# The first MoE's second matmul in rounded high and low parts one token tile earlier, in a fused kernel of scan, MoE and routed MoE

## The chip, the cores and the metric

The kernel is one program on one NeuronCore of a Trainium2 chip. The core has a matrix engine (TensorE, rows of the profile call it PE, its weight loads PEld), a vector engine (DVE), an activation engine (ACT), GpSimd (POOL) and a queue engine (SP) that starts most DMAs. Each engine works through its own instruction queue in order; semaphores tie the queues together. The metric is device time in microseconds, lower is better. The engines' times below are microseconds from the start of the span, unless ns is written.

## The reference

Three stages run one behind the other on 3072 tokens (4 sequences of 768) of width 256. The first is a gated linear scan with 8 heads, in chunks of 32. Its output goes to a dense MoE, and that to a routed MoE with 8 experts, of which each token takes the best one:

```
h = x @ w_in                     # 3072x256 @ 256x2048
g = h * np.cos(h)
x = g @ w_out                    # 3072x2048 @ 2048x256
...
logits = x @ w_gate
expert_idx = np.argmax(logits, axis=1)
...
h = np.maximum(np.einsum('ecd,edf->ecf', disp, w1), 0.0)
y = np.einsum('ecf,efd->ecd', h, w2)
...
out[i] = gate_w[i] * y[expert_idx[i], pos[i]]
```

The change concerns `x = g @ w_out`.

## The kernel before

**The first MoE.** The 3072 tokens are six tiles of 512 (`NT` = 6), and the 2048 hidden columns are 16 blocks of 128 (`NF` = 16). One block of one tile is an *item*, 96 in all; items 0 to 15 are tile 0, items 16 to 31 tile 1, and so on. For each item PE computes h (`mm1`, line 919, six matmuls of 512 columns in fp32r into the PSUM tile `hp`, of which there are three). Then ACT rounds (`c_round`, line 926, into one of six buffers named `g`), DVE takes the fraction (`c_frac`, line 930), ACT takes the sine (`c_sin`, line 933) and DVE multiplies by h (`c_mul`, line 936), which also gives `hp` back.

**The second matmul** (`mm2`) adds the item to the tile's output `yt`. It has two forms. For items below `SPLIT0` it is plain fp32: two matmuls of `w_out` on g (line 962), which the trace shows as four records. From `SPLIT0` on ACT first makes a rounded copy of g in fp32r, the high part (`c_hi`, line 940, tile `gh`), then `c_lo` (line 945) subtracts it to make the low part (`gw`, a buffer of the ring of `g`), and `mm2` is six fp32r matmuls (line 957: four on `gh`, two on `gw`) on `w_o`, which holds w_out in high and low parts. Before, `SPLIT0` is 32: tiles 0 and 1 are plain.

**What runs beside it.** The scan works in 12 groups of 256 tokens, about two for each tile (`a_...`). Per group ACT switches its table, takes an exponential of 2304 columns (line 644) and switches back (ACT_TABLE_LOAD rows at 644 and 933). w_in and w_out are loaded into `pre`, joined from words by DVE (`w_c1` to `w_c3`, lines 871 to 881) into `w_f`, a view of the memory that later holds `w1a`, and split into high and low parts (w_in: 890 on ACT, 894 on POOL; w_out: `w_ohi` 899 on ACT, `w_olo` 903 on POOL). `w_o` takes the memory of `pre`. After each tile its routing runs (`r_evac` evacuates `yt` at 970 and 976, `r_x2` matmuls at 990 and 992, `r_cp` 1006 and 1009, and more), and the expert weights are scaled and split (1229 to 1254) for the routed MoE, which takes the last 150 us or so.

**What sets the order.** The table `PLACE` gives every step, by name, a number for each of its occurrences; the steps are sorted by it and issued in that order. Each engine's queue holds its share of that one list.

Of the kernel before, what the change touches and what calls it, by code (L numbers as in the profile page):

```python
# [28 lines left out]
    'ass': [484, 563, 675, 815, 911, 1033, 1162, 1258],  # L29
# [51 lines left out]
    'chi': [617, 636, 640, 664, 666, 687, 712, 723, 739, 753, 763, 789, 790, 810, 826, 825, 869,  # L81
# [6 lines left out]
    'clo': [629, 658, 652, 677, 682, 713, 727, 729, 751, 776, 769, 794, 804, 812, 828, 842, 877,  # L88
# [5 lines left out]
    'con': [102],  # L94
    'cp': [176, 321, 371, 452, 597, 684, 801, 927, 1073, 1206],
    'css': [1500, 1536, 1580, 1604, 1640, 1655, 1683, 1723],
# [5 lines left out]
    'dfi': [236, 205, 243, 220, 342, 279, 297, 326],  # L102
    'et': [1377],
    'et2': [1393],
    'ete': [1416],
    'ets': [1402],
    'ett': [1406],
    'ex': [94, 115, 116, 151, 118, 233, 334, 362, 345, 430, 516, 545, 559, 667, 721, 830, 770,
        931, 928, 1047],
    'ex0': [1450],  # L110
    'ex1': [1623],
    'exp': [159, 260, 344, 444, 562, 679, 800, 908, 1028, 1157],
    'frc': [136, 146, 172, 190, 196, 209, 224, 240, 255, 281, 287, 306, 304, 313, 349, 360, 381,
# [6 lines left out]
    'gat': [138, 230, 323, 429, 540, 649, 798, 906, 1017, 1158],  # L120
    'id': [1469],
    'in0': [1475],
    'in1': [1629],
    'iv0': [1474],
    'iv1': [1732, 1737, 1742],
    'lt': [1552],
    'lte': [1610],
    'lts': [1568],
    'ltt': [1587],
# [203 lines left out]
def fused_kernel(ctx: ExitStack, tc: tile.TileContext, I, out: bass.AP):  # L333
# [10 lines left out]
    NF = 16  # L344
# [119 lines left out]
    at = at_cm.__enter__()  # L464
# [1267 lines left out]
    used = []  # L1732
# [77 lines left out]
```

## Time and profile before

| what | before |
|---|---|
| median of 3 runs | 575.1 us (573.28 to 575.87) |
| the profiled execution | 572.15 us |
| its span, first to last instruction | 570.4 us |
| PE busy | 533.9 us (94%) |
| DVE, ACT, POOL busy | 407.7 (71%), 371.5 (65%), 341.8 (60%) us |
| mean granted TensorE clock | 0.985 |

The share of PE is high over nearly all of the span, but matmul records overlap and their ends are modelled, so a busy PE may still wait a little between matmuls. A row of the chain of waits is one step of the work that ended last, followed back from the end of the program; a "window" row gives busy time of each engine in a stretch.

### The profile page before, as it was taken

Reading aid. Unit: us, or ns where it says so; the run is one execution under the profiler, and the core shown is the slowest. Engines: PE = TensorE matmul, PEld = TensorE weight load, DVE = VectorE, ACT = ScalarE, POOL = GpSimd, SP = SyncE. Lnnn points to the kernel's source line nnn. Section 1 sums busy time; section 2 is a strip of 40 time slices with the busy share of each in tenths; the row PEclk is TensorE's granted clock in tenths of the full one; section 3 lists DMA queues with packets and bytes.
Section 4 is the critical chain, followed back from the end, with each engine's and each line's share of the span. In section 5 each row is a group of like instructions: output and inputs, shape, how many; then the busy total and the mean of one; then the engine's idle time right before and its main releaser. Section 6 shows DMA issues by size and latency. Waiting matters only on the chain.

```text
span 570.4 us, 10385 instructions
## 1 busy us (share of the span) xinstructions
PE 533.9 (94%) x3156; PEld 385.5 (68%) x3156; DVE 407.7 (71%) x869; ACT 371.5 (65%) x675; POOL 341.8 (60%) x414
## 2 busy tenths in 40 slices
PE   8968999999999899999999997996989999999993
PEld 7635666666677678878888885674657665666672
DVE  7889985657876987699788799989966723333441
ACT  4638997684779597978798895787679622232220
POOL 6775152558558869776964773787568444322454
PEclk9999999999999999999999998999889999999997
DMA  7896744396263365326422231456897778777882
GB/s 241 260 328 234 235 146 126 119 333 196 95 203 114 110 203 185 130 81 197 153 70 75 75 110 39 130 144 176 187 206 189 127 147 152 141 143 117 155 171 63
DMA packets 110645, 89.91 MB, mean 158 GB/s; under 512 B 64542, under 2 KB 99424, under 8 KB 110592
## 3 DMA queue, kind: packets, MB, share of 16 engines
q1 hardware_dynamic: 107808, 82.26, 53.3%
q0 software_dynamic: 2784, 6.97, 5.0%
q8 instruction: 30, 0.49, 0.4%
q14 instruction: 23, 0.19, 0.1%
HBM read 59.50 MB, written 15.54 MB: 132 GB/s over the span
## 4 chain that ended last, share of the span: by engine, by line
PE 54%; DVE 17%; ACT 13%; DMA 9%; issue 5%; POOL 1%; SPq 0%; DVEq 0%; ACTq 0%; POOLq 0%
PE hp L919 16%; PE yt L962 8%; PE hp L1601 8%; PE yp L1648 7%; PE yt L957 7%; DMA ht<-hr 5%; DVE g L936 2%; DMA out_dram<-yacc,scat 2%; ACT g L933 2%; DVE g L930 2%; PE bcp L698 2%; ACT g L926 2%; DMA wst<-in_w_dram 1%; PE ypg L824 1%; PE sp L745 1%
## 5 line engine op out<-in xcount | busy, mean ns | idle before, releaser
L919 PE MATMUL hp<-xT,w_in 128*128 128x512 f32 x576 | 158.4, 414 | 6.7 <-DVE g L936 5.8
L919 PEld LDWEIGHTS hp<-xT,w_in 128*128 128x128 f32 x576 | 105.5, 189 | 39.7 <-DVE g L936 11.3
L945 POOL TENSOR_TENSOR gw<-g,gh 128x512 fp32r<-128x512 f32 x64 | 85.9, 1347 | 45.3 <-ACT gh L940 21.1
L933 ACT ACTIVATE g<-g,halfpi 128x512 f32<-128x512 f32 x96 | 68.2, 717 | 25.0 <-DVE g L930 24.4
L930 DVE SCALAR_TENSOR_TENSOR g<-g,hp 128x512 f32<-128x512 f32 x96 | 64.9, 680 | 27.1 <-ACT g L926 26.7
L1607 ACT ACTIVATE hr<-hp 128x512 f16<-128x512 f32 x58 | 33.5, 598 | 74.9 <-DMA ht<-hr 43.5
L1648 PEld LDWEIGHTS <-ht 128*128 128x128 f16 x696 | 68.2, 99 | 20.3 <-DMA ht<-hr 1.3
L936 DVE TENSOR_TENSOR g<-hp,g 128x512 f32<-128x512 f32 x96 | 65.2, 685 | 19.1 <-ACT g L933 19.1
L1611 DVE SCALAR_TENSOR_TENSOR hr<-hp,hr 128x512 f16<-128x512 f32 x58 | 39.1, 686 | 55.5 <-ACT hr L1607 51.2
L926 ACT ACTIVATE g<-hp 128x512 f32<-128x512 f32 x96 | 55.0, 588 | 30.6 <-PE hp L919 28.1
L957 PE MATMUL yt<-gh,w_o 128*128 128x512 f32 x256 | 70.8, 398 | 0.0
L962 PE MATMUL yt<-g,w1a 128*128 128x512 f32 x128 | 59.9, 597 | 3.3 <-DVE g L936 3.3
L957 PEld LDWEIGHTS yt<-gh,w_o 128*128 128x128 f32 x256 | 46.9, 188 | 9.0
L940 ACT ACTIVATE gh<-g 128x512 fp32r<-128x512 f32 x64 | 39.1, 623 | 12.1 <-DVE g L936 6.3
L1648 PE MATMUL yp<-w2a,ht 128*128 x348 | 44.9, 277 | 0.2
L1648 PE MATMUL yp<-w2b,ht 128*128 x348 | 43.7, 272 | 0.7 <-DMA ht<-hr 0.7
L1533 POOL DMA_INDIRECT xr<-xs_d,gat x29 | 31.3, 1079 | 20.9 <-DVE yacc L1662 4.9
L627 POOL TENSOR_TENSOR ex<-ex,ncum 128x512 f32<-128x512 f32 x32 | 35.3, 1122 | 11.7 <-DMA ex<-cumc_d 11.7
L1655 POOL TENSOR_TENSOR sc<-gall,invb 128x1 f32<-128x1 f32 x58 | 13.7, 247 | 45.6 <-ACT yacc L1660 24.4
L957 PE MATMUL yt<-gw,w_o 128*128 128x512 f32 x128 | 39.9, 393 | 0.3 <-POOL gw L945 0.2
L962 PEld LDWEIGHTS yt<-g,w1a 128*128 128x128 f32 x128 | 23.3, 189 | 24.3 <-issue 19.0
L1667 POOL DMA_INDIRECT out_dram<-yacc,scat x29 | 28.8, 994 | 18.1 <-DVE yacc L1662 9.8
(243 smaller groups left out, 990.9 us busy)
## 6 DMA issues: line engine op xcount, KB each, us to landing
wst<-in_w_dram SPq DMA_DIRECT2D x32, 512.0 KB
ex<-cumc_d SPq DMA_DIRECT2D x10, 1024.0 KB
pre<-in_w_io_dram SPq DMA_DIRECT2D x14, 512.0 KB
hl_d<-hl SPq DMA_DIRECT2D x10, 512.0 KB
b<-hl_d SPq DMA_DIRECT2D x10, 512.0 KB
c4s<-hl_d SPq DMA_DIRECT2D x40, 128.0 KB
xb<-in_xB_dram SPq DMA_DIRECT2D x11, 384.0 KB
xs_d<-xs SPq DMA_DIRECT2D x6, 514.0 KB
```

Of the source, the lines that this page charges most:

```text
L919: nc.tensor.matmul(hp, w_in[:, f, wl, k, :], xT[:, k, xl, :], start=(n == 0), stop=(n == 5))
L926: nc.scalar.activation(g, HP[it], AF.Copy, bias=MAGIC + 0.25)
L930: nc.vector.scalar_tensor_tensor(g, g, MAGIC, HP[it], op0=ALU.subtract, op1=ALU.subtract)
L933: nc.scalar.activation(GT[it], GT[it], AF.Sin, scale=SIN_SCALE, bias=halfpi)
L936: nc.vector.tensor_tensor(GT[it], HP.pop(it), GT[it], op=ALU.mult)
L940: nc.scalar.activation(h, GT[it], AF.Copy)
L945: eng.tensor_tensor(l, GT.pop(it), GH[it][0].bitcast(F32), op=ALU.subtract)
L957: nc.tensor.matmul(YT[t][k], WO['w'][:, f, o, k * P:(k + 1) * P], r, start=(f == 0 and n == 0), stop=(f == NF - 1 and n == 2))
L962: nc.tensor.matmul(YT[t][k], w_out[:, f, k * P:(k + 1) * P], g, start=(f == 0), stop=(f == NF - 1))
L1601: nc.tensor.matmul(hp, XK[i][:, 2 * xl + k, :], w[:, bass.ds(ev[i], 1), k, wl, :].rearrange("p a b -> p (a b)"), start=(n == 0), stop=(n = ...
L1611: nc.vector.scalar_tensor_tensor(hr[:, 1], HPB.pop(j), 0.0, hr[:, 0], op0=ALU.max, op1=ALU.subtract)
L1648: nc.tensor.matmul(yp, ht[:, hk, :], w[:, bass.ds(e, 1), k, wl, :].rearrange("p a b -> p (a b)"), start=(k == 0 and n == 0), stop=(k == 3 ...
```

## The change

Three things change; what is computed does not, up to rounding. `SPLIT0` becomes 16, so the 16 items of tile 1 take the form in parts: 64 plain records on PE (32 matmuls) become 96 fp32r matmuls, and 16 `c_hi` on ACT and 16 `c_lo` are new. Of these `c_lo` the eight with even block number run on POOL, as all the later ones do, and the eight with odd number on DVE. And `PLACE` is new throughout, of which two lines stand here:

```diff
-    'woh': [316, 347, 401, 388, 517, 338, 464, 492, 519, 422, 553, 495, 558, 489, 441, 509],
...
+    'woh': [312, 320, 336, 373, 356, 341, 392, 409, 413, 425, 375, 459, 506, 503, 447, 539],
...
     NIT = NT * NF
-    SPLIT0 = 2 * NF
+    SPLIT0 = NF
...
         if it >= SPLIT0:
             put('chi', c_hi, it)
-            put('clo', c_lo, it, GP)
+            put('clo', c_lo, it, V if t == 1 and f % 2 else GP)
```

Outside tile 1 and the steps that make `w_o`, the sequence of steps is nearly kept: most stand within ten places of where they stood. Line numbers of the changed kernel are two higher from the table on, so line 957 there is 959.

On PE, in the first third of tile 1, from the second matmul of item 17 to the first matmul of item 24; before:

```order
L962 MATMUL yt<-g,w1a 128x512 x2
L990 MATMUL xp<-idwg,yT 128x136
L992 MATMUL xp<-idwg,yT 128x136
L919 MATMUL hp<-xT,w_in 128x512 x12
L962 MATMUL yt<-g,w1a 128x512 x2
L990 MATMUL xp<-idwg,yT 128x136
L992 MATMUL xp<-idwg,yT 128x136
L962 MATMUL yt<-g,w1a 128x512 x4
L745 MATMUL sp<-c4s,b_1099 128x256 x4
L1233 MATMUL pn<-wsc,ones_f 128x1
L919 MATMUL hp<-xT,w_in 128x512 x6
```

PE in the change, from the second matmul of item 17 to that of item 19:

```order
L959 MATMUL yt<-gh,w_o 128x512 x4
L959 MATMUL yt<-gw,w_o 128x512 x2
L959 MATMUL yt<-gh,w_o 128x512 x4
L959 MATMUL yt<-gw,w_o 128x512 x2
L992 MATMUL xp<-idwg,yT 128x136
L994 MATMUL xp<-idwg,yT 128x136
L921 MATMUL hp<-xT,w_in 128x512 x6
L747 MATMUL sp<-c4s,b_1172 128x256 x4
L921 MATMUL hp<-xT,w_in 128x512 x6
L959 MATMUL yt<-gh,w_o 128x512 x4
L959 MATMUL yt<-gw,w_o 128x512 x2
```

The first matmul of item 24 (the last `hp` row of each) stood behind the second matmuls of items 17 to 20; now it stands behind those of 17 and 18 alone, and 19 and 20 follow it.

On ACT at the same place, around the exponential of a scan group, from the first `w_o` row behind the round of item 19 to the sine of item 21; before:

```order
L899 ACTIVATE w_o<-w1a 128x256
L933 ACTIVATE g<-g,halfpi 128x512
L926 ACTIVATE g<-hp 128x512
L1006 ACTIVATE x_1016<-xp 128x264
L1009 ACTIVATE xs,n_1017<-x_1016 128x256
L899 ACTIVATE w_o<-w1a 128x256
L644 ACT_TABLE_LOAD
L644 ACTIVATE ex<-ex 128x2304
L1229 ACTIVATE w1a,wsc<-wst_1008 128x2x512
L926 ACTIVATE g<-hp 128x512 x2
L933 ACT_TABLE_LOAD
L933 ACTIVATE g<-g,halfpi 128x512
```

ACT in the change, from the high part of item 18 to the sine of item 21:

```order
L942 ACTIVATE gh<-g 128x512
L1008 ACTIVATE x_1021<-xp 128x264
L1011 ACTIVATE xs,n_1022<-x_1021 128x256
L942 ACTIVATE gh<-g 128x512
L901 ACTIVATE w_o<-w1a 128x256
L646 ACT_TABLE_LOAD
L646 ACTIVATE ex<-ex 128x2304
L901 ACTIVATE w_o<-w1a 128x256
L928 ACTIVATE g<-hp 128x512 x2
L835 ACTIVATE xT<-ypg 128x2x256
L935 ACT_TABLE_LOAD
L935 ACTIVATE g<-g,halfpi 128x512
```

High parts now stand in front of the exponential (that of item 17 two rows ahead of these, those of 18 and 19 here), the copy `xT` has moved from behind the sine to ahead of the second table load, the square of `w1a` has moved ahead of the round of item 20, and of the four rounds that stood between the round of item 19 and the sine of item 21 the last (that of item 23) has moved behind that sine.

On DVE in the change, the place of the first of the eight low parts (item 17):

```order
L932 SCALAR_TENSOR_TENSOR g<-g,hp 128x512
L938 TENSOR_TENSOR g<-hp,g 128x512
L783 TENSOR_TENSOR tmp<-up,hmask 128x256
L784 SCALAR_TENSOR_TENSOR st<-st,ex,tmp 128x256
L938 TENSOR_TENSOR g<-hp,g 128x512
L947 TENSOR_TENSOR gw<-g,gh 128x512
```

Before, no `gw` row stands in the queue of DVE at all; here one stands behind the multiplication of item 20 and ahead of the routing's and the next items' steps.

## Rows read from the trace of the kernel before

**Rows 1.** The page: busy shares, and PE and its granted clock in 40 slices.

```profile
PE 533.9 (94%) x3156; PEld 385.5 (68%) x3156; DVE 407.7 (71%) x869; ACT 371.5 (65%) x675; POOL 341.8 (60%) x414
...
PE   8968999999999899999999997996989999999993
...
PEclk9999999999999999999999998999889999999997
```

**Rows 2.** Windows: us, busy time and records of PE, PEld, DVE, ACT, POOL; clock, DMA.

```profile
60.00:80.00 20.00, 20.00 (x105) 13.34 (x104) 18.91 (x33) 18.75 (x39) 6.94 (x9) 1.00 0.51 173
104.00:165.00 61.00, 60.84 (x291) 39.77 (x290) 45.70 (x101) 41.89 (x75) 36.34 (x43) 1.00 0.62 198
165.00:225.00 60.00, 57.86 (x334) 47.02 (x334) 48.03 (x105) 47.06 (x80) 45.96 (x44) 1.00 0.49 156
225.00:280.00 55.00, 54.85 (x320) 44.74 (x320) 45.67 (x102) 44.74 (x76) 41.69 (x41) 1.00 0.41 128
```

**Rows 3.** The same windows view, second matmuls alone (line 962, then line 957).

```profile
104.20:164.00 59.80, 29.82 (x64) 11.50 (x64) 1.00 0.61 197
...
164.00:224.70 60.70, 24.99 (x96) 17.77 (x97) 1.00 0.50 157
```

**Rows 4.** Chain of waits, tile 1 and then tile 2: start us, us, what.

```profile
135.18 1.72 PE yt L962 x4
136.90 1.38 PE hp L919 x6
...
195.92 1.38 PE yt L957 x6
```

**Rows 5.** One line's instructions: duration ns min/median/max, first and last start us.

```profile
L940 ACT ACTIVATE gh<-g x64: 611/622/635, 159.8 to 377.6; 128x512 fp32r<-128x512 f32 x64
...
L945 POOL TENSOR_TENSOR gw<-g,gh x64: 1274/1296/2292, 160.5 to 378.3; 128x512 fp32r<-128x512 f32 x64
...
L936 DVE TENSOR_TENSOR g<-hp,g x96: 673/684/693, 40.4 to 375.6; 128x512 f32<-128x512 f32 x96
...
L876 DVE SCALAR_TENSOR_TENSOR w1a<-pre,w1a x14: 675/684/2268, 10.2 to 74.6; 128x512 int32<-128x512 int32 x14
...
L1035 DVE SCALAR_TENSOR_TENSOR xs<-x,n,xs x24: 467/478/1518, 122.6 to 392.3; 128x256 f16<-128x256 f32 x24
```

**Rows 6.** Groups of instructions in 104 to 165: busy us, mean ns, idle before.

```profile
L933 ACT ACTIVATE g<-g,halfpi 128x512 f32<-128x512 f32 x17 | 12.0, 714 | 2.2 <-DVE g L930 2.2
L926 ACT ACTIVATE g<-hp 128x512 f32<-128x512 f32 x17 | 9.8, 590 | 14.8 <-PE hp L919 14.8
...
L899 ACT ACTIVATE w_o<-w1a 128x256 fp32r<-128x256 f32 x11 | 3.9, 404 | 0.0
...
L833 ACT ACTIVATE xT<-ypg 128x512 fp32r<-128x512 f32 x2 | 1.2, 579 | 0.0
...
L903 POOL TENSOR_TENSOR w_o<-w1a,w_o 128x256 fp32r<-128x256 f32 x14 | 11.2, 806 | 4.7 <-ACT w_o L899 4.7
```

**Rows 7.** Chain of waits in 106 to 125, around the first exponential of tile 1.

```profile
106.03 1.50 PE hp L919 x6
...
107.56 0.60 ACT g L926
...
113.43 2.13 ACT ex L644
...
118.88 0.72 ACT g L933
...
120.11 0.69 DVE xT L836
...
123.47 1.50 PE hp L919 x6
```

**Rows 8.** Timeline of ACT around the second exponential of tile 1.

```profile
145.43 2.15 ACT L644 ACTIVATE ex<-ex 128x2336 f32<-128x2336 f32 x1
...
149.86 0.72 ACT L933 ACTIVATE g<-g,halfpi 128x512 f32<-128x512 f32 x1
```

More of the change, by code (lines that the diff above doesn't have):

```diff
@@ L23 @@
 PLACE = {
[5 rows of a table removed]
-    'ass': [484, 563, 675, 815, 911, 1033, 1162, 1258],
[51 rows of a table removed]
-    'chi': [617, 636, 640, 664, 666, 687, 712, 723, 739, 753, 763, 789, 790, 810, 826, 825, 869,
[6 rows of a table removed]
-    'clo': [629, 658, 652, 677, 682, 713, 727, 729, 751, 776, 769, 794, 804, 812, 828, 842, 877,
[5 rows of a table removed]
-    'con': [102],
-    'cp': [176, 321, 371, 452, 597, 684, 801, 927, 1073, 1206],
-    'css': [1500, 1536, 1580, 1604, 1640, 1655, 1683, 1723],
[5 rows of a table removed]
-    'dfi': [236, 205, 243, 220, 342, 279, 297, 326],
-    'et': [1377],
-    'et2': [1393],
@@ L105 @@
[L105 to L113, printed above, removed]
[6 rows of a table removed]
[L120 to L129, printed above, removed]
[20 rows of a table removed]
-    'mul': [141, 156, 183, 194, 211, 219, 248, 253, 276, 294, 296, 324, 337, 335, 367, 378, 391,
[15 rows of a table removed]
[5 rows of a table added]
+    'ass': [505, 593, 714, 827, 940, 1068, 1188, 1292],
[51 rows of a table added]
+    'chi': [401, 430, 436, 485, 442, 510, 500, 536, 535, 553, 571, 579, 608, 626, 630, 635, 647,
[7 rows of a table added]
+    'clo': [407, 456, 455, 494, 477, 524, 521, 541, 538, 567, 572, 595, 615, 627, 640, 652, 660,
[6 rows of a table added]
+    'con': [100],
@@ new lines @@
+    'cp': [188, 327, 352, 483, 628, 726, 836, 965, 1093, 1224],
+    'css': [1523, 1570, 1609, 1639, 1670, 1687, 1709, 1747],
[5 rows of a table added]
+    'dfi': [206, 212, 232, 236, 345, 285, 302, 328],
+    'et': [1404],
+    'et2': [1427],
+    'ete': [1446],
+    'ets': [1431],
+    'ett': [1438],
+    'ex': [67, 116, 114, 159, 115, 240, 203, 390, 476, 493, 590, 597, 603, 738, 769, 849, 816,
+        954, 870, 1082],
+    'ex0': [1472],
+    'ex1': [1658],
+    'exp': [163, 256, 347, 451, 586, 719, 829, 942, 1064, 1199],
@@ L166 @@
+    'frc': [131, 143, 173, 191, 200, 207, 229, 243, 262, 283, 292, 317, 310, 321, 360, 366, 396,
[6 rows of a table added]
+    'gat': [148, 230, 350, 466, 585, 713, 838, 944, 1049, 1185],
+    'id': [1513],
+    'in0': [1502],
+    'in1': [1667],
+    'iv0': [1499],
+    'iv1': [1756, 1757, 1762],
+    'lt': [1592],
+    'lte': [1643],
+    'lts': [1607],
+    'ltt': [1623],
[20 rows of a table added]
+    'mul': [139, 152, 179, 199, 208, 222, 248, 257, 276, 294, 308, 330, 354, 335, 367, 377, 400,
[15 rows of a table added]
     'p15': [21],
[4 rows of a table removed]
[4 rows of a table added]
     'p2': [8],
[2 rows of a table removed]
[2 rows of a table added]
     'p22': [10],
[1 row of a table removed]
[1 row of a table added]
@@ L178 @@
     'p26': [9],
[13 rows of a table removed]
[13 rows of a table added]
     'p39': [38],
[1 row of a table removed]
[1 row of a table added]
     'p40': [33],
[38 rows of a table removed]
[38 rows of a table added]
     'p78': [77],
[1 row of a table removed]
[1 row of a table added]
     'p8': [3],
[19 rows of a table removed]
-    'raw': [58, 242, 355, 425, 567, 681, 795, 947, 1008],
[4 rows of a table removed]
-    'rev': [395, 398, 624, 632, 868, 870, 1087, 1091, 1294, 1298, 1486, 1488],
-    'rex': [1202, 1367, 1546],
-    'rg1': [539, 749, 998, 1197, 1331, 1529],
-    'rg2': [593, 809, 1040, 1262, 1376, 1551],
-    'rh0': [466, 659, 913, 1153, 1348, 1510],
-    'rh2': [498, 744, 955, 1226, 1355, 1520],
-    'rl0': [475, 715, 926, 1168, 1356, 1514],
-    'rl2': [616, 813, 1012, 1270, 1366, 1531],
@@ L268 @@
-    'rnd': [135, 127, 157, 189, 186, 199, 223, 237, 245, 274, 275, 305, 298, 312, 348, 357, 377,
[10 rows of a table removed]
-    'rst': [630, 880, 1051, 1295, 1386, 1570],
-    'rx0': [402, 638, 875, 1095, 1308, 1492],
-    'rx1': [411, 639, 874, 1093, 1306, 1493],
-    'rx2': [449, 695, 918, 1142, 1315, 1498],
-    'rx3': [433, 691, 922, 1108, 1300, 1495],
-    's0': [175, 206, 267, 307, 350, 368, 465, 457, 589, 579, 701, 759, 832, 863, 953, 949, 1080,
-        1068, 1211, 1212],
-    's1': [171, 201, 291, 266, 364, 369, 487, 476, 578, 615, 703, 755, 836, 852, 973, 980, 1048,
-        1066, 1176, 1174],
@@ L288 @@
-    'sin': [137, 153, 174, 192, 200, 212, 246, 249, 264, 282, 290, 315, 317, 325, 361, 375, 386,
[6 rows of a table removed]
-    'sml': [91],
-    'sph': [56, 97, 285, 370, 473, 619, 745, 823, 961, 1037],
-    'spi': [112, 179, 314, 414, 533, 648, 777, 850, 988, 1089],
-    'spl': [68, 103, 302, 403, 524, 641, 764, 844, 978, 1065],
-    'st': [216, 376, 336, 372, 417, 427, 554, 570, 680, 694, 740, 784, 886, 864, 1001, 1025,
-        1058, 1165, 1205, 1432],
-    'u': [188, 318, 332, 346, 389, 419, 488, 521, 670, 668, 718, 783, 858, 862, 966, 986, 1050,
-        1146, 1203, 1312],
@@ L303 @@
-    'ud': [1256, 1318, 1330, 1411],
-    'uh': [1293, 1349, 1404, 1471],
-    'ul': [1311, 1325, 1388, 1384, 1441, 1431, 1491, 1479],
-    'un': [1259, 1326, 1374, 1426],
-    'used': [1812],
-    'uss': [1281, 1338, 1400, 1453],
[7 rows of a table removed]
-    'wih': [63, 134, 162, 158, 177, 193, 213, 218, 247, 273, 270, 299, 309, 322],
-    'wil': [78, 147, 163, 160, 182, 198, 228, 221, 254, 292, 277, 303, 329, 327],
-    'wld': [113, 96, 120, 105, 123, 84, 185, 217, 180, 215, 207, 241],
-    'woh': [316, 347, 401, 388, 517, 338, 464, 492, 519, 422, 553, 495, 558, 489, 441, 509],
@@ L320 @@
-    'wol': [352, 448, 522, 477, 527, 494, 514, 518, 596, 523, 569, 511, 611, 607, 581, 706],
-    'x': [128, 232, 259, 416, 538, 599, 678, 780, 962, 1134],
-    'yg': [251, 339, 423, 557, 683, 773, 904, 1004, 1114, 1219],
-    'zero': [467],
[19 rows of a table added]
+    'raw': [65, 275, 353, 468, 599, 717, 822, 945, 1048],
[4 rows of a table added]
+    'rev': [402, 403, 658, 661, 889, 895, 1113, 1123, 1328, 1329, 1517, 1520],
+    'rex': [1245, 1405, 1576],
+    'rg1': [565, 783, 1016, 1232, 1359, 1567],
+    'rg2': [625, 846, 1083, 1295, 1421, 1578],
@@ new lines @@
+    'rh0': [479, 689, 957, 1192, 1370, 1535],
+    'rh2': [502, 775, 984, 1280, 1385, 1557],
+    'rl0': [497, 745, 967, 1195, 1384, 1545],
+    'rl2': [648, 847, 1039, 1299, 1397, 1581],
+    'rnd': [130, 137, 158, 181, 180, 197, 223, 242, 246, 278, 277, 315, 304, 319, 349, 351, 379,
[10 rows of a table added]
+    'rst': [662, 923, 1122, 1300, 1434, 1599],
+    'rx0': [406, 675, 901, 1127, 1332, 1521],
+    'rx1': [432, 670, 912, 1132, 1330, 1522],
+    'rx2': [471, 712, 953, 1167, 1352, 1540],
+    'rx3': [450, 706, 917, 1139, 1334, 1537],
@@ new lines @@
+    's0': [169, 218, 269, 306, 358, 382, 487, 480, 589, 606, 728, 786, 869, 893, 995, 974, 1107,
+        1088, 1225, 1235],
+    's1': [171, 201, 279, 272, 365, 370, 518, 515, 598, 644, 737, 765, 879, 884, 1007, 1021,
+        1087, 1098, 1207, 1209],
+    'sin': [135, 149, 174, 194, 205, 217, 244, 254, 268, 287, 300, 322, 323, 324, 361, 374, 397,
[6 rows of a table added]
+    'sml': [87],
+    'sph': [58, 93, 288, 371, 491, 650, 789, 845, 998, 1063],
+    'spi': [109, 160, 348, 423, 556, 707, 797, 891, 1030, 1133],
+    'spl': [69, 102, 301, 394, 537, 665, 796, 872, 1026, 1121],
@@ new lines @@
+    'st': [220, 299, 337, 368, 411, 452, 580, 624, 715, 724, 766, 819, 915, 960, 1031, 1054,
+        1102, 1196, 1243, 1479],
+    'u': [183, 291, 329, 340, 380, 434, 526, 558, 699, 703, 735, 807, 890, 909, 993, 1042, 1094,
+        1190, 1222, 1419],
+    'ud': [1276, 1349, 1400, 1455],
+    'uh': [1325, 1371, 1435, 1506],
+    'ul': [1344, 1351, 1408, 1409, 1476, 1463, 1515, 1530],
+    'un': [1287, 1360, 1411, 1461],
+    'used': [1863],
+    'uss': [1312, 1369, 1429, 1486],
[7 rows of a table added]
+    'wih': [64, 136, 166, 161, 182, 190, 214, 215, 251, 281, 271, 289, 293, 309],
@@ L324 @@
+    'wil': [70, 147, 170, 168, 189, 209, 231, 216, 253, 297, 273, 311, 331, 333],
+    'wld': [113, 103, 127, 108, 140, 86, 162, 219, 195, 224, 196, 245],
+    'woh': [312, 320, 336, 373, 356, 341, 392, 409, 413, 425, 375, 459, 506, 503, 447, 539],
+    'wol': [313, 334, 343, 386, 378, 381, 393, 435, 443, 446, 453, 484, 520, 507, 522, 614],
+    'x': [125, 226, 305, 420, 562, 638, 778, 833, 990, 1180],
+    'yg': [250, 344, 438, 583, 716, 806, 932, 1043, 1147, 1265],
+    'zero': [499],
 }
```

438 rows, old and new, of the table PLACE are left out of this document.

## The prediction

> **What bounds the kernel now.** I read the page first. PE is busy 94% of the span, and its line of 40 slices is nearly all nines between slice 5 and slice 23 at a clock granted in full [rows 1]: the first MoE, in which the change lies, runs at PE's pace at first sight. To see what that pace is made of I took the chain of waits next. In most of tile 1 it walks along PE alone: a first matmul of an item takes 1.38 us, a plain second one 1.72 us, and the second one in parts, as tile 2 has it, 1.38 us [rows 4]. The windows then give the length of a stage. The 64 plain records of tile 1 fill 104.2 to 164.0, and the 96 records of tile 2 start right behind and end by 224.7 [rows 3]; so a stage is 60.5 us in tile 1 and 60 us in tile 2, and the window to 280 shows 55 us for tile 3 [rows 2]. The reader should stop here: tile 2 has 5.4 us less of second matmul than tile 1 and is yet hardly shorter. PE's pace isn't all. In tile 2 PE is busy 57.86 of 60.00, in tile 1 60.84 of 61.00 [rows 2].
>
> Inside tile 1 there is one long stretch that isn't PE's. From 107.56 to about 123.47 the chain runs on ACT, through the round, the table switch, the exponential of a scan group (2.13 us) and the sine at 118.88, then through DVE back to PE [rows 7]. Elsewhere ACT has time: in 104 to 165 it waited 14.8 us for PE's first matmuls [rows 6].
>
> **The change part by part.** *PE's work.* Sixteen items change from 1.72 to 1.38 us [rows 4]: 16 x 0.34 = 5.4 us less, all on the engine that the chain follows through most of the tile. That is the most that this edit gives; nothing else in the change removes work.
>
> *Work added beside it.* ACT: 16 x 0.62 = 10.0 us. POOL: 8 x 1.30 = 10.4 us. On DVE the trace shows no `gw`; the nearest row is the multiplication of the same size, 0.68 us, and 8 x 0.68 = 5.5 us [rows 5]. It is a lower bound: the multiplication has one input in PSUM, `gw` has both in SBUF. For that the nearest rows are line 876 and line 1035 with medians of 0.68 and 0.48 us, but slowest ones of 2.27 and 1.52 [rows 5], 1.0 to 1.6 us above. So eight of them cost DVE 5.5 us at best and, with each as late as the slowest of these, 5.5 + 8 x 1.6 = 18.3. I take 7, since the medians of both lines lie at their minimum and the late ones are few.
>
> What the sum does if the late ones are many is told by a rule. The Trainium skill's "SBUF — State Buffer", section "SBUF: two separate sides", says that a VectorE instruction with two SBUF inputs and a GpSimd instruction that reads SBUF exclude each other for the whole of an instruction; POOL's 1.30 us in front of each `gw` would make it 8 x 1.98 = 15.8 us by that rule. The trace agrees that it can happen (the maxima above, and 2.29 us for a `gw` on POOL of median 1.30) and not that it is usual. It speaks against this change, and is the slower rival below.
>
> *Is there room?* Tile 1 had DVE at 45.70, ACT at 41.89 and POOL at 36.34 of 61.00 us [rows 2]. Fourteen of the sixteen `w_o` subtractions ran in it [rows 6]; in the new order seven stand ahead of the first `gw`, so some five move into tile 0, where POOL has room, and take 5 x 0.81 = 4.0 us along. With a stage of 56 us this makes DVE 45.7 + 7 = 52.7 (94%), ACT 51.9 (93%) and POOL 42.7 (76%). The window 60 to 80 shows that it can be: there DVE is at 18.91 and ACT at 18.75 of 20.00 while PE is busy throughout [rows 2]. But tile 2 was held up with DVE at 48.03 and ACT at 47.06 of 60.00 [rows 2], so shares decide nothing; the places do.
>
> *The first exponential.* Up to the sine of item 21 the new queue of ACT has in addition three high parts (17, 18, 19), one more `w_o` and the copy `xT`, and has lost a round and a sine: 3 x 0.62 + 0.40 + 0.58 - 0.59 - 0.71 = 1.5 us more [rows 5, 6]. A good part of it lies ahead of round 20, where ACT sat and waited for the first matmul that ended at 107.5 [rows 7], so I take the sine of 21 to end at about 120 instead of 119.6. DVE's subtraction for `xT`, which stood ahead of the multiplication at 120.11 [rows 7], no longer has to wait there; the multiplication ends at 120.7 and the first matmul of item 24, which needs the buffer that it frees, at 122.1. Now the second matmuls of 19 and 20 stand behind it on PE, where they stood ahead: 122.1 + 2 x 1.38 = 124.9. Before, PE was at the same point at 123.47 + 1.50 = 125.0 [rows 7]. Five items changed form by then, worth 1.7 us, and 0.1 is left: 1.6 us is lost, as PE runs out of work while ACT is in its block.
>
> *The second exponential* stands at 145.43, and the sine behind it ends at 150.6 [rows 8]. In the new order all of ACT's block can start earlier, because PE reaches the first matmuls ahead of it sooner. But the second matmul of item 28 needs a high part that stands behind that sine and then a low part on POOL, 0.62 + 1.30 us [rows 5], where the plain one needed neither. PE has the second matmul of 27 (1.38) in between, so some 0.6 us of waiting is left.
>
> *Everything else at nothing.* The `w_o` steps must be early: POOL was busy 6.94 of 20.00 in 60 to 80 [rows 2] and covers them; if it didn't, tile 1 would begin late by up to 0.81 for each that is missing. The six buffers of the ring hold g and `gw` both, as in tiles 2 to 5. The steps of other tiles keep their neighbours, and where they don't I see no side on which they err; I allow 1.5 us either way. What becomes late next is tile 2's own beginning, which waits for tile 1's output and moves with it.
>
> *The sum.* -5.4 + 1.6 + 0.6 = -3.2 us. The profiled execution of 572.15 us would be 569.0. It lies 2.95 below the median of the three runs, 575.1, and I carry the difference over to that: **571.9 us**.
>
> **The rivals.** *PE's pace throughout* (569.7). The first block is less tight than I make it, and the full 5.4 us come out. For it: the window 60 to 80 with two engines at 94% and PE without a gap [rows 2], and that ACT waited 14.8 us for PE in tile 1 [rows 6]. Against it: the chain at 107.56 to 123.47 [rows 7].
>
> *Tile 1 becomes a second tile 2* (574.0, 573.2 to 575.1). ACT, DVE and POOL now hand every item around six times instead of four, and the stage is set by that and not by PE. For it: tile 2, in parts, took 60 us with loads no greater [rows 2, 3]; a stage of the same 60 us gives 0.5 us. Against it: tile 3 does the same matmuls in 55 [rows 2], and tile 2 has its own first groups of the split to take in. I put its middle at 1.1 us won.
>
> *Slower: DVE and POOL in each other's way* (578.5). Place: the eight `gw` on DVE, each in front of the next item's fraction and multiplication, which give back `hp`. If each waits for a POOL instruction of 1.30 us, DVE's tile is 45.7 + 15.8 = 61.5 us, more than the 60.5 of the whole stage now, and the same wait falls on POOL where DVE is first. A tile of 62 to 64 us, 1.5 to 3.5 longer and no gain from PE, gives 576.6 to 578.6, and 578.5 where the low parts on POOL are late as well. It decides where the mean wait passes about 1 us, half as much again as the instruction itself. Against it: medians at the minimum [rows 5]. By the Trainium skill's rule cited above this is the normal case wherever POOL reads SBUF; its median here says otherwise.
>
> **How the numbers follow.** Chances: the forecast (570.7 to 573.2) 0.40; PE's pace throughout 0.24; a second tile 2 0.26; slower 0.10. Half a percent, 2.9 us, is about what a measurement of this kernel can tell from no change. The forecast lies near that bound, so I split its 0.40 into 0.26 faster and 0.14 the same; with PE's pace the faster side has 0.50. The second tile 2 goes to the same, 0.26, as does 0.02 of the slower case: 0.42, and 0.08 for slower. For the range I take PE's pace with 1.5 us for the moved steps, 568.2, and on the other side no change with somewhat under 1 us of the runs' own spread, 575.9; out of it fall most of the slower case and the edge of the best one.
>
> **What would show it.** Line 959 of the profile after has 384 + 96 = 480 records, and the chain shows six of them in 1.38 us in tile 1 as well; line 964 has 64. Right is the sum if the stage of tile 1, from its first second matmul to that of tile 2, is 57 to 58 us, with a gap on PE of about 3 us ahead of the first matmul of item 24 and a wait on POOL's `gw` near 150. It is PE's pace if the stage is 55 to 56 us. It is the second rival if the chain in tile 1 runs mostly on ACT and DVE, and the slower one if `gw` on DVE has a mean over 1.6 us. I am wrong in another way if tile 1 gains what I say and the end doesn't: then a later tile gave it back, and its window in the profile must be longer than here.

## The result, and the profile after

The changed kernel takes 569.41 us (median of 8 runs, 566.53 to 570.96) where the kernel before takes 575.29 (8 runs beside it): a ratio of 0.9896, with a 95% interval from 0.9869 to 0.9924. Run again it took 569.73, ratio 0.9911 [0.9875, 0.9947]. Its profiled execution took 568.56 us, with a span of 566.8. The forecast was 571.9 with a range of 568.2 to 575.9, and 569.0 for the profiled execution.

The page of the changed kernel, busy shares and PE in 40 slices:

```profile
PE 528.7 (93%) x3188; PEld 387.9 (68%) x3188; DVE 415.7 (73%) x877; ACT 379.2 (67%) x691; POOL 355.6 (63%) x422
...
PE   8778999999999999999999998899589999998993
...
PEclk9999999999999999999999998999789999999998
```

Against [rows 1], PE has lost 5.2 us of busy time, and DVE, ACT and POOL have gained 8.0, 7.7 and 13.8. The clock is granted in full from tile 1 to tile 4, as it was.

Line 959 has the 480 records forecast (320 on `gh`, 160 on `gw`) and line 964 has 64. Where the time went is seen by cutting the first MoE into stages, each from the first second matmul of a tile to that of the next. Here are the second matmuls in parts (line 959) in the windows of tiles 1 to 4: window, its length, PE busy with that line and records, clock, DMA share and GB/s.

```profile
103.20:161.90 58.70, 25.59 (x96) 1.00 0.56 189
161.90:219.60 57.70, 24.35 (x96) 1.00 0.49 157
219.60:274.60 55.00, 24.24 (x96) 1.00 0.42 134
274.60:328.00 53.40, 24.38 (x96) 1.00 0.34 100
```

The same view of a second trace of the kernel before (run `r2_before_again`, below), tile 1 by line 962 and tiles 2 to 4 by line 957. It repeats the stages of the first trace within 0.1 us.

```profile
105.60:166.30 60.70, 29.86 (x64) 1.00 0.63 200
...
166.30:226.20 59.90, 25.00 (x96) 1.00 0.51 154
226.20:281.30 55.10, 24.57 (x96) 1.00 0.42 129
281.30:332.60 51.30, 23.87 (x96) 1.00 0.34 104
```

The reader should see three things. Tile 1 went from 60.7 to 58.7, so 2.0 us of the 5.4 that PE saves. Tile 2, whose form didn't change, went from 59.9 to 57.7. And tile 4 went from 51.3 to 53.4 and gave back 2.1.

Inside tile 1, this is the chain of waits of the changed kernel around the first exponential (start us, us, what), the place of [rows 7]:

```profile
110.83 1.28 ACT L646
...
112.13 0.36 ACT ex L646
...
117.33 0.72 ACT g L935
...
118.60 0.61 DVE g L938
119.21 0.04 issue
119.25 1.66 PE hp L921 x6
120.91 1.38 PE yt L959 x6
...
122.40 1.49 PE yt L959 x6
123.89 2.73 PE hp L921 x12
```

The chain still goes through ACT here, over the table load, the sine and the multiplication on DVE, to a first matmul, and two second matmuls now stand behind that. The timeline of PE shows all of its gaps in that block (start us, us, instruction, and in brackets the idle time before it):

```profile
117.50 0.50 PE L747 MATMUL sp<-c4s,b 128*128 128x256 f32 x2 [0.42 <-DVE xT L838]
118.58 0.50 PE L747 MATMUL sp<-c4s,b 128*128 128x256 f32 x2 [0.58 <-DVE rsm L1003]
119.25 1.66 PE L921 MATMUL hp<-xT,w_in 128*128 128x512 f32 x6 [0.17 <-DVE g L938]
```

### The profile page after: what moved, and what is told of

The parts are those of the page before. It is cut to its first block, busy times and chain, and to the rows that moved or that the text cites. A ratio compares the mean times of both kernels' runs of the same rounds, so it can differ in the third digit from the quotient of the medians.

```text
span 566.8 us, 10500 instructions
## 1 busy us (share of the span) xinstructions
PE 528.7 (93%) x3188; PEld 387.9 (68%) x3188; DVE 415.7 (73%) x877; ACT 379.2 (67%) x691; POOL 355.6 (63%) x422
## 4 chain that ended last, share of the span: by engine, by line
PE 45%; DVE 25%; ACT 11%; DMA 7%; issue 6%; POOL 3%; SPq 1%; POOLq 0%; ACTq 0%; DVEq 0%
PE hp L1603 10%; PE hp L921 9%; PE yp L1650 9%; PE yt L959 7%; DVE g L938 4%; DVE g L932 3%; ACT g L935 3%; DMA out_dram<-yacc,scat 2%; PE yt L964 2%; ACT ex L646 2%; ACT g L928 2%; DVE w2a L1256 1%; DVE xs L1037 1%; POOL out_dram L1669 1%; ACT gh L942 1%
## 5 line engine op out<-in xcount | busy, mean ns | idle before, releaser
L921 PE MATMUL hp<-xT,w_in 128*128 128x512 f32 x576 | 153.7, 406 | 4.7 <-DVE g L938 2.5
L947 POOL TENSOR_TENSOR gw<-g,gh 128x512 fp32r<-128x512 f32 x72 | 98.8, 1376 | 47.6 <-ACT gh L942 22.8
L959 PE MATMUL yt<-gh,w_o 128*128 128x512 f32 x320 | 88.4, 398 | 0.1
L935 ACT ACTIVATE g<-g,halfpi 128x512 f32<-128x512 f32 x96 | 67.9, 717 | 27.0 <-DVE g L932 26.4
L959 PEld LDWEIGHTS yt<-gh,w_o 128*128 128x128 f32 x320 | 58.3, 188 | 12.7 <-issue 1.0
L942 ACT ACTIVATE gh<-g 128x512 fp32r<-128x512 f32 x80 | 48.7, 622 | 11.0 <-DVE g L938 6.5
L959 PE MATMUL yt<-gw,w_o 128*128 128x512 f32 x160 | 50.9, 399 | 1.6 <-POOL gw L947 0.8
L1535 POOL DMA_INDIRECT xr<-xs_d,gat x29 | 34.3, 1181 | 20.0 <-DMA xk<-xr 7.5
L629 POOL TENSOR_TENSOR ex<-ex,ncum 128x512 f32<-128x512 f32 x32 | 37.5, 1193 | 3.3 <-DMA ex<-cumc_d 2.1
L1664 DVE SCALAR_TENSOR_TENSOR yacc<-yp,sc,yacc 128x256 f32<-128x256 f32 x29 | 13.5, 481 | 32.3 <-PE yp L1650 23.6
L959 PEld LDWEIGHTS yt<-gw,w_o 128*128 128x128 f32 x160 | 29.5, 189 | 11.1 <-POOL gw L947 3.3
```

The lines of the kernel that those rows point to most:

```text
L629: nc.gpsimd.tensor_tensor(lt, lt, nn, op=ALU.add)
L921: nc.tensor.matmul(hp, w_in[:, f, wl, k, :], xT[:, k, xl, :], start=(n == 0), stop=(n == 5))
L935: nc.scalar.activation(GT[it], GT[it], AF.Sin, scale=SIN_SCALE, bias=halfpi)
L942: nc.scalar.activation(h, GT[it], AF.Copy)
L947: eng.tensor_tensor(l, GT.pop(it), GH[it][0].bitcast(F32), op=ALU.subtract)
L959: nc.tensor.matmul(YT[t][k], WO['w'][:, f, o, k * P:(k + 1) * P], r, start=(f == 0 and n == 0), stop=(f == NF - 1 and n == 2))
```

## The experiments

Each ran beside the kernel before on one chip (three chips in all), and its ratio is to that. "Tile n" is a stage as above, in the profiled execution.

**The order alone** (`e1_order_alone`): the changed kernel with tile 1 plain, and the 32 numbers of its high and low parts taken out of the table.

```diff
-    SPLIT0 = NF
+    SPLIT0 = 2 * NF
```

> The new order of all steps, but tile 1 keeps the plain second matmul (its sixteen high and sixteen low parts are left out of the list). Three theories. (1) The prediction's: the split itself gives about 3 us net and the order gives nothing, so 575 +- 1 here. (2) The order does most of the 5.9 us between the medians: 571 or less here. (3) The split gives its full 5.4 us, part of it inside tile 1 and the rest in tile 2: the order gives nothing or little, 574 to 576 here, and the trace shows tile 2 no shorter than the 60 us of the kernel before.

574.72 us, ratio 1.0001 [0.9970, 1.0032]. The windows of its second matmuls, tile 1 (plain), then tiles 2 and 4:

```profile
103.90:164.90 61.00, 29.75 (x64) 1.00 0.56 190
...
164.90:222.40 57.50, 24.36 (x96) 1.00 0.49 148
...
277.40:330.80 53.40, 24.38 (x96) 1.00 0.33 100
```

The gain of tile 2 and the loss of tile 4 are the order's, whole; in tile 1 the order changes little (61.0 against 60.7). Some 0.5 us of tile 2's gain is moved and not saved: four records of the routing's matmuls (`xp`) now lie in tile 3. By its median the new order taken as a whole is worth nothing that can be measured; what the tail of the trace has to do with that is said at the last two runs.

**The form alone** (`e2_split_alone`): the kernel before with `SPLIT0 = NF` and the low parts shared out as in the change. The new steps, those of `w_o` and the second matmuls of tile 1 stand at places worked out from the new table; all else has its old place.

```diff
-    SPLIT0 = 2 * NF
+    SPLIT0 = NF
...
-            put('clo', c_lo, it, GP)
+            put('clo', c_lo, it, V if t == 1 and f % 2 else GP)
```

> The old order, but tile 1's second matmul in parts; only its own steps (high and low parts, the sixteen second matmuls, the making of w_o) stand where the new order has them relative to their neighbours, the odd low parts on the vector engine. (1) The split gives about 3 us: 572. (2) The order does most: 573 to 575. (3) The full 5.4 us come out: 569.5 to 570.5.

591.69 us, ratio 1.034 [1.0291, 1.0390]. Tile 1 took 75.2 us. What PE waited for in 103 to 142 (waiter, what it waited for, us in all, times, longest), and windows of 10 us (PE, PEld, DVE, ACT, POOL busy; clock):

```profile
PE sp L658 <- DVE xT L749: 4.9, 1, 4.9
PE yt L870 <- POOL gw L858: 2.2, 1, 2.2
PE hp L832 <- DVE g L849: 1.7, 1, 1.7
```

```profile
120.00:130.00 10.00, 4.67 (x22) 3.66 (x20) 3.05 (x6) 9.10 (x14) 5.41 (x8) 0.93 0.64 159
130.00:140.00 10.00, 9.46 (x35) 7.58 (x34) 5.21 (x16) 5.86 (x13) 4.29 (x7) 0.73 0.70 274
140.00:150.00 10.00, 8.83 (x40) 7.05 (x39) 8.48 (x11) 4.94 (x9) 6.50 (x7) 1.00 0.18 61
```

In 120 to 130 ACT is at 9.10 of 10.00 and DVE and PE stand idle behind it: this is ACT's block around the exponential, and the scan's matmuls (line 658; lines here are 89 lower than in the change) wait on PE for the copy `xT`, which stands behind the sine of that block. The block comes late: its table load is 14.4 us into the tile (at 119.66), where it was 8.0 before and is 7.6 in the change. PE had waited 2.2 us for a low part on POOL, and the high part ahead of the block 2.3 us for a multiplication on DVE. The form needs an order with more room for it than these places give; they aren't the best that the old order could have had. The clock is a second loss: PE was busy less than half of the first window at a granted clock of 0.93, and in the second the clock was 0.73, a mean of its two levels of 1.2 and 2.4 GHz.

**PE's saving without the added work** (`e5_pe_alone`): the multiplication of tile 1 writes g rounded, and all six second matmuls read that.

```diff
     def c_mul(it):
+        if it // NF == 1:
+            r = mq.tile([P, T], F32R, tag="g", name="gr", bufs=6)
+            nc.vector.tensor_tensor(r, HP.pop(it), GT.pop(it), op=ALU.mult)
+            GH[it] = [r, r]
...
-        if it >= SPLIT0:
+        if t == 1:
+            seen['chi'] = seen['clo'] = f + 1
+        elif it >= SPLIT0:
```

> The changed kernel without the added work: in tile 1 the multiplication writes the rounded value itself, and the six matmuls of an item all read that; the sixteen high parts on the activation engine and the sixteen low parts are left out, so tile 1 loses its low part. PE does the same six matmuls. (1) The added work costs 2.2 us of PE's 5.4 in the stretches around the two exponentials: about 2 us less than the changed kernel, 567 to 567.5. (2) and (3) The added work lies beside PE for nothing: 569 to 570, no difference from the changed kernel.

564.01 us, ratio 0.9828 [0.9790, 0.9867]. That is 3 us below the lowest theory and 5.4 below the change; its tile 1, shown below, is 2.7 us shorter than the change's, so half of that distance isn't located.

**The added work without PE's saving** (`e6_added_alone`): high and low parts are made and not used.

```diff
-        if it >= SPLIT0:
+        if t > 1:
             h, l = GH.pop(it)
```

> The changed kernel with the added work and without PE's saving: in tile 1 the high and low parts are made and not used, and the second matmul is the plain one. (1) PE has 5.4 us more to do and the exponentials' stretches are longer: the order-alone run plus 1 to 2 us, 576 to 577. (2) 573 to 574, the order's gain less a little. (3) The added work is free: the order-alone run within 0.7 us, about 575.

576.68 us, ratio 1.0051 [1.0018, 1.0084], as the first theory had it.

**High parts without low ones** (`e8_no_low`), which leaves out the low parts' buffers of the ring too:

```diff
-            for n, (o, r) in enumerate(((0, h), (1, h), (0, l))):
+            for n, (o, r) in enumerate(((0, h), (1, h), (1 if t == 1 else 0, l))):
...
-            put('clo', c_lo, it, V if t == 1 and f % 2 else GP)
+            if t == 1:
+                seen['clo'] = f + 1
+            else:
+                put('clo', c_lo, it, GP)
```

> The changed kernel without the sixteen low parts of tile 1: its third pair of second matmuls reads the high part a second time, against the low part of w_out, so PE, the order and the high parts stay and the result of tile 1 loses the low part of g. Theory: of the 2.6 us that the added work costs in tile 1, most is ACT's, whose three high parts stand ahead of the first exponential; then the tile stays near 58.0 us (58.7 in the change, 56.1 without any added work) and the end is about 0.7 us earlier than the change's (569). Rival: it is the low parts, by POOL and DVE in each other's way or by the hand-over from ACT to POOL to PE; then the tile falls to 56.3 to 56.7 us and the end to 566 to 567.

569.60 us, ratio 0.9903 [0.9874, 0.9933], which can't be told from the change. The windows of tile 1 in these three, in their order:

```profile
103.20:159.20 56.00, 24.58 (x96) 1.00 0.57 193
```

```profile
103.90:166.50 62.60, 29.75 (x64) 1.00 0.53 177
```

```profile
102.70:159.80 57.10, 24.77 (x96) 1.00 0.58 194
```

With one order throughout, tile 1 is thus 61.0 us plain, 56.0 with PE's saving alone, 57.1 with the high parts too, 58.7 with all. PE's saving is 5.0, the high parts cost 1.1 of it and the low parts 1.6. Added to plain items the work costs 62.6 - 61.0 = 1.6. Neither theory on `e8_no_low` was right: the cost is shared. The starts of the second matmuls in the three traces tell where. From item 16 to item 20 the change takes 19.0 us, `e8_no_low` 19.0 and `e5_pe_alone` 17.7: the first 1.3 us are the high parts', at the first exponential. From item 20 to item 32 it is 39.7, 38.1 and 38.4: all the rest is the low parts'.

**All low parts on POOL** (`e3_all_pool`) **and all of tile 1's on DVE** (`e4_all_dve`):

```diff
-            put('clo', c_lo, it, V if t == 1 and f % 2 else GP)
+            put('clo', c_lo, it, GP)
```

```diff
-            put('clo', c_lo, it, V if t == 1 and f % 2 else GP)
+            put('clo', c_lo, it, V if t == 1 else GP)
```

> The changed kernel with all sixteen low parts of tile 1 on POOL, at the same places of the list. If the eight on the vector engine pay for sharing with POOL (the rival 'slower' of the prediction), this is faster by up to 2 us, with tile 1's stage below 58.7 us. If they are worth their place, since one on the vector engine takes 0.69 and one on POOL 1.30 us and each stands ahead of a second matmul, tile 1's stage is 60 to 61 us and the time 1 to 2 us above the changed kernel's.

> The changed kernel with all sixteen low parts of tile 1 on the vector engine. It is busy 52.0 of the 61 us from 104 to 165 already; eight more of 0.69 us are 5.5 us. If tile 1 is held by the order in which engines hand items on and not by one engine's load, the stage stays within 1 us of 58.7. If the vector engine is the next bound, it grows by 2 to 4 us, to 61 to 62.5.

580.62 us, ratio 1.0112 [1.0065, 1.0159], and 577.22, ratio 1.0025 [0.9995, 1.0054]. Tile 1 took 69.7 and 65.2 us, several us more than any theory gave. What PE waited for in tile 1 (us in all, times, longest), all on POOL first, then all on DVE, then the change:

```profile
PE yt L959 <- POOL gw L947: 6.8, 5, 3.6
```

```profile
PE yt L959 <- DVE gw L947: 4.4, 3, 2.2
PE hp L921 <- DVE g L938: 2.1, 2, 1.4
```

```profile
PE yt L959 <- DVE gw L947: 0.5, 2, 0.3
```

In the change PE waits 0.5 us for low parts; here it waits 6.8 for those on POOL, and 4.4 for those on DVE with 2.1 more for DVE's multiplications. With all on POOL the granted clock of the tile was also 0.95 instead of 1.00, and PE was busy 60.8 us instead of 56.9. The busy share of an engine wouldn't have told it: in 122 to 142 DVE is busy 18.83 of 20.00 us in the change and 18.50 with all low parts on DVE. At these places the sharing is worth 11.0 and 6.5 us of this tile, more than PE's saving; I had taken it for a detail. Other places for the low parts weren't tried.

**The old order from tile 4 on** (`e7_hybrid`): the steps behind the first second matmul of tile 4 in their old sequence, as in this row of the table:

```diff
-    'ah': [532, 612, 730, 854, 946, 1125, 1202, 1302],
+    'ah': [532, 612, 730, 854, 946, 1125, 1199, 1303],
```

> The changed kernel's order up to the first second matmul of tile 4, and from there the order of the kernel before. In the traces the new order takes 57.6 us for tile 2 where the old takes 60.0, and 53.4 for tile 4 where the old takes 51.3, whatever form tile 1 has. If both belong to the order of those tiles themselves, tile 4 is back at 51.3 us here and the time about 2 us under the changed kernel's, near 567. If tile 4's loss is a debt that the new tile 2 or 3 leaves behind, tile 4 stays at 53 us and the time doesn't change.

570.55 us, ratio 0.9937 [0.9905, 0.9969]. Tile 4 stayed at 53.2. The two orders put first matmuls at different places between the second ones, so only stretches with the same work on PE can be compared: items 64 to 72 (48 records of first matmuls in each) and 72 to 80 (42). From the second matmul of item 64 to that of item 72 this run took 28.73 us, the kernel before 26.75 and the change 26.62; from 72 to 80 it took 24.52, the kernel before 24.52 and the change 26.73. So the loss of tile 4 lies in its second half, and the old order doesn't have it there. The seam costs this run 2.1 us in the first half, where PE once waits 1.5 us for a multiplication on DVE, and so it gives back what it wins. Whether it pays a debt there or only for the seam it doesn't tell.

**One step moved away from a meeting of DVE and POOL** (`e9_low_moved`), **and a second one** (`e10_two_moved`):

```diff
-    'rl2': [648, 847, 1039, 1299, 1397, 1581],
+    'rl2': [648, 847, 1039, 1292.500, 1397, 1581],
```

```diff
-    'rl2': [648, 847, 1039, 1299, 1397, 1581],
+    'rl2': [648, 847, 1039, 1292.500, 1403.500, 1581],
```

> The changed kernel with one step moved: the subtraction for the low part of tile 3's second half in its routing stands before the steps of the gate instead of behind them. Theory: tile 4 is 2 us longer in the new order (53.4 against 51.3 us) because the two DVE instructions of line 1037 at 315.6 stood beside two of POOL and took 2.77 us where 0.88 is usual; parted from them, tile 4 takes 51.5 to 52.0 us and the end is 1.5 us earlier (568). Rival: the loss belongs to the order of many steps together, or another pair meets in its place; tile 4 stays at 53 us or more and the end at 569.5.

> As the run before, and the same step of tile 4 moved behind its neighbour on DVE. Theory of the meeting of DVE and POOL: the subtraction at 339.8, 2.58 us there and 0.88 alone, no longer meets three low parts on POOL; another 1.0 to 1.7 us, the last second matmul at 372.5 instead of 375.7 and the end at 566 to 567. Rival, that these instructions have slack or meet the next ones: the last second matmul stays at 374 or later and the end at that of the run before.

In tile 4 of the changed kernel the chain walks along DVE from 305 to 319. Its timeline there has two rows that are far too long, and POOL's has these beside them:

```profile
308.24 1.22 DVE L1090 TENSOR_SCALAR rsm<-rsm 128x4 f32<-128x4 f32 x1
...
315.56 2.77 DVE L1037 SCALAR_TENSOR_TENSOR xs<-x,n,xs 128x256 f16<-128x256 f32 x2
```

```profile
308.14 1.29 POOL L947 TENSOR_TENSOR gw<-g,gh 128x512 fp32r<-128x512 f32 x1 [1.88 <-ACT w1a L1231]
...
315.49 1.29 POOL L947 TENSOR_TENSOR gw<-g,gh 128x512 fp32r<-128x512 f32 x1 [3.41 <-ACT gh L942]
316.76 1.29 POOL L1252 TENSOR_SCALAR w1a<-wst,wsc 128x1024 f16<-128x1024 f32 x1
```

In the kernel before, where the pair's line is 1035, it took the usual time:

```profile
319.24 0.88 DVE L1035 SCALAR_TENSOR_TENSOR xs<-x,n,xs 128x256 f16<-128x256 f32 x2
```

With the step moved (its lines are 89 lower) the pair takes 0.87, and two small instructions stand at the old place:

```profile
313.81 0.87 DVE L948 SCALAR_TENSOR_TENSOR xs<-x,n,xs 128x256 f16<-128x256 f32 x2
...
315.24 0.94 DVE L1015 TENSOR_TENSOR rsm<-rsm 128x4 f32<-128x4 f32 x1
316.21 1.07 DVE L1016 COPY xs<-rsm 128x4 f32<-128x4 f32 x1
```

```profile
314.86 1.29 POOL L858 TENSOR_TENSOR gw<-g,gh 128x512 fp32r<-128x512 f32 x1 [3.42 <-ACT gh L853]
316.13 1.12 POOL L1163 TENSOR_SCALAR w1a<-wst,wsc 128x1024 f16<-128x1024 f32 x1
```

Both end within 0.03 us of the POOL instruction beside them, and take 0.17 us in the change. So the meeting costs nearly the same whoever meets: the pair wins 1.90 and these two lose 1.67. Tile 4 went to 52.9, not to 51.5 to 52, and the time was 569.60, ratio 0.9892 [0.9845, 0.9938], the same as the change. The second move didn't help either: 571.14, ratio 0.9912 [0.9882, 0.9942]; the last second matmul came 2.2 us later than in the change, not 3.2 earlier, and 1.6 of that in tile 5, in which the step stands.

That DVE and POOL hold each other up there is shown; that this is the 2.1 us of tile 4 isn't, and the cause stays open. The traces point to many such meetings together: in items 72 to 80 the DVE instructions that run more than 0.15 us over the median of their kind add up to 3.3 us over it in the change and 3.1 with the step moved, and to 0.4 in the kernel before and in `e7_hybrid`, which don't lose there. DVE was busy 12.89 of 14.00 us in 305 to 319, and 10.94 in the same stretch of the tile before (310.3 to 324.3).

**Both kernels again** (`r1_changed_again`, `r2_before_again`), no edit:

> The changed kernel once more, for a second trace. At the last second matmul of the first MoE the first trace was 3.2 us ahead of the kernel before, the medians differ by 5.9. If what stands before the routed MoE repeats from run to run, the stages here agree within 0.5 us with the first trace (58.7, 57.6, 55.0, 53.4 us for tiles 1 to 4), and only the part behind 376 us moves; if not, the stages differ by more than 1 us, and differences between single traces of that size say nothing.

> The kernel before, once more, for a second trace. If what the medians differ by beyond the 3.2 us at the last second matmul (5 to 6 us in all) is that the first profiled execution was a quick one of its kind, then its stages agree with the first trace within 0.5 us, tile by tile, and behind the last second matmul it takes 193 to 194 us instead of 191.5. If the first trace stands for the kernel, that tail is 191.5 again, and the difference lies elsewhere. The ratio to itself is 1.000.

569.73 us, ratio 0.9911 [0.9875, 0.9947], and 575.15, ratio 1.0005 [0.9975, 1.0036]. The stages of both repeat within 0.5 us. The second trace of the kernel before has a span of 573.9 instead of 570.4: tile 1 starts 1.5 us later, and from the start of the last second matmul to the end it takes 193.6 us instead of 191.6. The changed kernel's two traces have 191.1 and 192.7 there. So that tail, mostly the routed MoE, varies by 2 us from run to run in one and the same kernel; over all fourteen traces it takes 190.3 to 195.8. It was longest, 195.8 and 194.8, in `e1_order_alone` and `e6_added_alone`, which run level with the change for the first 105 us of it and lose 4 to 5 us in the next 50; why, I don't know. It goes with their medians, which lie further from the others than tile 1 does: 5.3 us separate `e1_order_alone` and the change, and tile 1 shows 2.3 of that. At the last second matmul `e1_order_alone` is 0.4 to 1.8 us ahead of the kernel before. So how the 1% is shared between form and order isn't settled by the medians; the stages show what is said above.

## Why the prediction was right, and where it wasn't

The forecast was right in sign and its range held the time. The two costs that it took from rows, PE's saving and the low parts on DVE, were right. The time of the profiled execution was met by luck, and the median came out 2.5 us lower for another reason.

*PE's work, -5.4 us.* Right: -5.0, from `e1_order_alone` against `e5_pe_alone`. The chain shows six records in 1.38 us in tile 1 too.

*The low parts on DVE, 7 us.* Right. Two groups of the changed kernel in 104 to 165 (busy us, mean ns):

```profile
L947 POOL TENSOR_TENSOR gw<-g,gh 128x512 fp32r<-128x512 f32 x10 | 13.2, 1324 | 7.1 <-DVE gw L947 3.1 <-ACT gh L942 2.9 <-POOL hl L553 0.6
...
L947 DVE TENSOR_TENSOR gw<-g,gh 128x512 fp32r<-128x512 f32 x8 | 7.7, 959 | 0.3 <-ACT gh L942 0.3
```

The eight took 7.7 us, with a median of 0.69. Five took 0.68 to 0.69, and three took longer, each beside a POOL instruction. These are the three, and then what ran on POOL when each began:

```profile
126.49 1.11 DVE L947 TENSOR_TENSOR gw<-g,gh 128x512 fp32r<-128x512 f32 x1
...
130.89 1.74 DVE L947 TENSOR_TENSOR gw<-g,gh 128x512 fp32r<-128x512 f32 x1
...
158.43 1.40 DVE L947 TENSOR_TENSOR gw<-g,gh 128x512 fp32r<-128x512 f32 x1
```

```profile
126.31 0.73 POOL L905 TENSOR_TENSOR w_o<-w1a,w_o 128x256 fp32r<-128x256 f32 x1
...
130.47 1.61 POOL L947 TENSOR_TENSOR gw<-g,gh 128x512 fp32r<-128x512 f32 x1 [0.62 <-POOL hl L553]
...
157.98 1.30 POOL L947 TENSOR_TENSOR gw<-g,gh 128x512 fp32r<-128x512 f32 x1 [1.12 <-ACT gh L942]
```

The mean of 0.96 is far below the 1.6 us of the slower rival. Each of the three ends 0.55 us behind the end of the POOL instruction beside which it began. Of the other five four had no POOL instruction beside them, and one began 0.17 us ahead of one and took its usual time. So the prediction's fear, POOL's 1.30 us in front of each, came to 0.42, 1.05 and 0.71 us in front of three. The Trainium skill's "SBUF — State Buffer", section "SBUF: two separate sides", which the prediction weighed, holds where two such instructions meet, as in these rows. The rule says what a meeting costs, and the order says how many there are.

*The first exponential, 1.6 us lost.* Right in size; the sign that it named was wrong. The prediction put the first matmul at 122.1 and the end of the two second ones behind it at 124.9. In the changed kernel they end at 120.91 and 123.89; tile 1 starts 0.9 us earlier there (103.25 against 104.15), so on the clock of the trace before this is 121.8 and 124.8. But PE's gaps in the block are 0.42 + 0.58 + 0.17 = 1.2 us, not 3, and most of that is in front of the scan's matmuls and not of the first matmul. By items, against `e5_pe_alone`, the loss from 16 to 24 is 31.53 - 29.65 = 1.9 us. A slip of names, here and in the section on the change: items were counted by their place in PE's queue; the first matmul that is called item 24's is item 25's in both kernels, since both orders exchange the two. The reading is the same.

*The second exponential, 0.6 us lost.* The size is near and the place wrong. From item 24 to 32 the change loses 27.2 - 26.4 = 0.8 us, by the low parts, as `e8_no_low` shows. But PE didn't wait for a `gw` of POOL near 150: its one wait in 143 to 162 is 0.2 us, for a `gw` of DVE.

*Everything else at nothing.* This step failed in its parts and held in its sum. The new order gives tile 2 2.4 us and takes 2.1 from tile 4, as `e1_order_alone` shows with the form undone. Tile 0 is 1.2 us longer, and its beginning is earlier: the first second matmul of tile 1 comes at 102.3 to 104.0 us in the eleven traces with the new order and at 104.2, 105.3 and 105.6 in the three with the old one. The sum at the last second matmul (375.7 us in the change, 378.9 and 380.3 in the two traces of the kernel before) is 3.2 to 4.6 us won, against the 3.2 forecast; tile 1 alone gave 2.0 of that. Against the first trace the 3.2 is 2.1 from an earlier start of tile 0, -1.2 in tile 0, 2.0 in tile 1, 2.4 in tile 2 and -2.1 in tile 4; that it meets the forecast is luck. The mark of 57 to 58 us for tile 1 was missed by 0.7 us, 1.2 from its middle: PE saved 0.4 less, the added work cost 0.5 more, and the order 0.3.

*The carry-over to the median.* Here the forecast lost its 2.5 us. For the profiled execution it said 569.0, and it was 568.56, by the luck told above. But it then added 2.95, as the profiled execution of the kernel before lay that far below its median, and the change's lies 0.85 below: a difference of 2.1, and with the 0.44 before it that is the 2.5. The second trace of before shows why: the first was a quick execution, by 1.5 us at its start and by 2 in the routed MoE. A quick start and a quick tail of one execution say nothing of the other kernel's next one. What I can't settle is how much of the 5 to 6 us between the medians is the stages' 3.2 to 4.6 and how much lies in tails: the interval of the ratio alone is 3 us wide.

*The rivals.* PE's pace throughout would have been `e5_pe_alone`'s 56.0 us for tile 1; the added work stood in its way. A second tile 2 went wrong in its premise: the 60 us of tile 2 weren't the form's, since the same form takes 57.5 in another order. That should have been a warning: a stage's length is its order's as much as its work's.

## What to carry to other kernels

When a faster form on the bounding engine brings work for its neighbours, cost the two apart: here 5.0 us were saved and 2.7 of them given back. Without a share for each of the two helper engines tile 1 was 11.0 and 6.5 us longer, and the change a loss (ratio 1.0112) or nothing that can be measured (1.0025); in the old order, at the places tried, it was a loss (1.034). Before a difference between a profiled execution and a median is carried over to another kernel, find out in which stage it lies, by a second trace. An order that gains in one tile can lose it in another; a table of stages with the form undone shows it at once. Before two orders are compared over a stretch, count that the bounding engine has the same work in it.

## What the runs showed of the hardware

- An instruction of DVE on 128x4 elements that takes 0.17 us alone took 0.94 to 1.22 beside a POOL instruction and ended together with it. Moving the long instruction away moved the wait to the short ones that came in its place. The Trainium skill's page named above has a section, "Who interferes with whom", by which copies and arithmetic with a scalar, which have one input, can be held up like this as well where their operands meet its conditions; lines 1090 (of the change) and 1016 (of `e9_low_moved`) are such instructions, and the trace agrees that both waited.
- In `e2_split_alone` the stretch of 10 us in which PE was busy 4.67 had a granted clock of 0.93, the next one 0.73, though PE was busy 9.46 of it again, and the one behind it 1.00. The long wait on PE was paid for once more after it had ended.
